# A top-32 attention and mixer kernel: sixty score blocks masked by an accumulating DMA, and one small VectorE step moved to GpSimd, in a newly planned order

## The chip, the core and the metric

The kernel runs on one core of a Trainium2 chip. The metric is device time in microseconds (us): the median of several executions. The engines are called PE (TensorE), DVE (VectorE), ACT (ScalarE), POOL (GpSimd) and SP (SyncE, which here only issues DMAs). Each works through its own list of instructions strictly in order; between engines they wait for each other by semaphores.

## What is computed

```python
scores = scale * np.matmul(q, k.transpose(0, 1, 3, 2))        # (8, 8, 576, 576)
kth = np.partition(scores, -32, axis=-1)[..., -32:-31]
scores = np.where(scores >= kth, scores, -1e9)                # keep the 32 largest of a row
attn = softmax(scores)                                        # with 1e-9 added to the sum
x = np.matmul(attn, v)  ->  (batch, seq, heads * 64)
h = np.maximum(x.T @ w_tok1, 0) @ w_tok2                      # mixing over tokens
u = x + h.T
out = u + np.maximum(u @ w_ch1, 0) @ w_ch2                    # mixing over channels
```

Batch 8, 8 heads, 576 tokens, head size 64, hidden sizes 256 (tokens) and 1536 (channels). The exact 32nd largest of each of 36,864 rows of 576 scores has to be found.

## The kernel before

**Tiles.** Heads go in 32 pairs. A pair's 2 x 576 rows make nine tiles of 128 rows, and two tiles make a duo, so there are 288 tiles in 144 duos, nine duos (`two(m)`) for each of 16 couples of pairs. A duo's scores are 128 partitions x 2 x 576.

**One duo (`scores`, `group`), in order of its data.** PE multiplies q and k into PSUM (L568, 16 matmuls). ACT copies the scores, scaled and shifted, into a buffer `SX` (L378). DVE takes the eight largest of each of seven segments of a row (L605, MAX8, fourteen for a duo) and merges them (L609, L610, L612) into a guess of the threshold, `thi`; `nh` is its negative (L705, a line that a helper `small` shares). ACT counts with the sign function how many scores lie above the guess (L621, into `cnt`). From the count come three small factors, 128x6 numbers each, all made on DVE at L705: `gs` (which side to search), `ws` (how far) and `as`, which is made from `ws`. POOL rewrites the scores in `SX` as whole numbers with `nh` and `gs` (L628, twice) and sets eight dummies behind each row with `as` (L631). One more DVE MAX8 over 584 numbers gives the exact threshold `tlo` (L637, twice), `nt` is its negative.

**Masking, in two ways.** 104 duos are "swap" duos: POOL writes a mask byte into `U` (L646, twice), PE adds it, made hugely negative, to a second computation of the scores in PSUM (L578 and L584, the "rescore"), and ACT takes the exponential out of PSUM into `Pm` (L651). The other 40 (the table `KEEP`, and every fifth duo of nine, whose rows come from both pairs) need no second computation: ACT takes the exponentials of the unmasked scores from `SX` early into `E` (L617), DVE makes two more small factors `no` (L659), POOL writes a mask of zeros and ones `M` (L663, twice) and multiplies (L668, twice) into `Pm`.

**Behind the mask.** SP issues a transposing DMA `Pm` to `PT` (L690); PE multiplies `PT` with v (L741); DVE divides by the row sums into `Xb` (L757, L760). When a batch's four pairs are done, `mlp_ops` runs its mixing on PE and ACT (L813 to L937, L889 for the last product, L907 for the copy out). PE fills some gaps with matmuls whose result nobody reads (`heat`, L1068). At the end `judge` and `sums` (DVE, L1030 to L1054) work out from counts and thresholds whether a slower exact path has to run; in these runs it doesn't.

**What sets the order.** Nothing is left to run time: `Plan.run` takes every operation with an engine, a duration, dependences, buffers and a due time (`DUE` and `SHIFT`, interpolated over the tiles) and lists, at build time, what stands when on each engine. The numbers in `DUE`, `SHIFT`, `TOL` and the durations in `plan.add` thus decide the order and nothing else.

**Buffers.** Ten `SX`, three `U`, eight `PT`, three `Pm`, two `E`, two `M`; PSUM has eight banks, a duo's scores or second scores hold four of them.

Of the kernel before, what the change touches and what calls it, by code (L numbers as in the profile page):

```python
# [31 lines left out]
KEEP = tuple(18 * m + 2 for m in range(16)) + tuple(18 * m + 14 for m in range(8))  # L32
# [4 lines left out]
    lq=-133.951, tq=-932.231, ck=-35.592, nh=237.787, vc=490.837, mm=-49.848, cp=-459.747, seg=521.49, rnd=1.494,  # L37
    sg=-30.872, g=136.538, a=154.386, w=-424.736, x=323.58, dum=1.612, mx=-190.096, nt=-286.048, u=-918.815,
    re=-1.774, ex=-191.301, ex1=16.779, tr=-511.689, pv=-52.864, nm=-625.622, mlp=94.104, seg1=-6.015, rnd1=278.031,
    x1=49.757, sg1=49.48, mx1=-334.781, pace=-2.756, mla=-161.079, first=-599.221, part=-502.53, rest=-442.515,  # L40
# [1218 lines left out]
```

## Time and profile before

| | |
|---|---|
| time, median of 3 runs | 753.7 us (753.56 to 754.14) |
| the profiled execution | 754.53 us, of which the core's span is 752.7 us |
| busy in the span | PE 709.1 us (94%), DVE 702.5 (93%), ACT 666.1 (88%), POOL 631.7 (84%) |
| TensorE clock granted | 0.997 of full speed over the span |
| DMA | 90.51 MB, mean 120 GB/s |

A busy time is the union of the times in which an engine had an instruction in flight. Instructions of one engine overlap, so the busy time of a group can be more than the engine's time that it costs; where that matters, starts of successive instructions are compared. The 1.8 us outside the span belong to every run.

### The profile page before, as it was taken

The numbers are of one execution on the slowest core, as the hardware profiler recorded it, in microseconds if no ns is written. First come the engines' busy times: TensorE is split into PE (matmuls) and PEld (weight loads), VectorE is DVE, ScalarE is ACT, GpSimd is POOL, SyncE is SP. The second block draws the span as 40 slices with busy tenths as digits, with TensorE's granted clock in tenths as the row PEclk, the third lists the DMA queues.
The fourth block names the chain that finished last, engine by engine and source line by source line (L and its number), as shares of the span: only waits on it lengthen the run. The fifth ranks groups of instructions, "written<-read, shape, count | busy, mean of one in ns | idle before, by whom it ended". The sixth has DMA issues, their size and how long they took to land.

```text
span 752.7 us, 23305 instructions
## 1 busy us (share of the span) xinstructions
PE 709.1 (94%) x7638; PEld 388.8 (52%) x7638; DVE 702.5 (93%) x4384; ACT 666.1 (88%) x1134; POOL 631.7 (84%) x859
## 2 busy tenths in 40 slices
PE   8888899999999999999999999999999999999995
PEld 3444545555555545554556555555555455555652
DVE  8999999999999999999999999999999999996620
ACT  5987989998999999999989999999998989997441
POOL 4799999999898999999997899999879897987300
PEclk9999999999999999999999999999999999999998
DMA  5865986975759557475676557688744747345521
GB/s 127 161 114 95 160 130 116 154 150 121 147 82 163 102 130 153 98 127 130 125 145 141 102 100 144 143 146 130 131 93 93 141 96 153 76 76 84 100 71 61
DMA packets 286722, 90.51 MB, mean 120 GB/s; under 512 B 273024, under 2 KB 283136, under 8 KB 286592
## 3 DMA queue, kind: packets, MB, share of 16 engines
q1 hardware_dynamic: 282768, 84.97, 59.5%
q0 software_dynamic: 3024, 3.77, 3.7%
q8 instruction: 62, 1.02, 0.6%
q14 instruction: 68, 0.56, 0.2%
q10 hardware_dynamic: 800, 0.20, 0.1%
HBM read 35.85 MB, written 9.44 MB: 60 GB/s over the span
## 4 chain that ended last, share of the span: by engine, by line
DVE 79%; PE 15%; ACT 2%; issue 1%; DMA 0%; SPq 0%; POOL 0%; ACTq 0%; POOLq 0%
DVE cd L605 34%; DVE tlo L637 23%; DVE cd L610 5%; PE bank L889 5%; DVE thi L612 4%; PE bank L937 3%; DVE m L609 3%; DVE Xb L760 2%; PE bank L584 2%; DVE nt L705 1%; DVE nh L705 1%; DVE ws L705 1%; PE bank L741 1%; ACT SX L378 1%; DVE as L705 1%
## 5 line engine op out<-in xcount | busy, mean ns | idle before, releaser
L605 DVE MAX8 cd<-SX 128x8 f32<-128x82 f32 (+1 forms) x2016 | 379.0, 231 | 1.9 <-ACT SX L378 1.7
L628 POOL TENSOR_SCALAR SX<-SX,nh,gs 128x576 int32<-128x576 f32 x288 | 234.7, 827 | 9.4 <-DVE as L705 3.8
L621 ACT ACTIVATE sg<-SX,nh 128x576 bf16<-128x576 f32 x288 | 223.1, 777 | 12.7 <-DVE nh L705 10.9
L637 DVE MAX8 tlo<-SX 128x8 uint32<-128x584 uint32 x288 | 219.0, 760 | 4.7 <-POOL SX L628 3.3
L646 POOL TENSOR_SCALAR U<-SX,nt,ws 128x576 uint8<-128x576 int32 x208 | 169.7, 831 | 22.0 <-DVE nt L705 5.4
L568 PE MATMUL bank<-kT,qT 64*64 64x288 f32 x2304 | 172.8, 414 | 11.4 <-ACT Pm L651 4.1
L378 ACT ACTIVATE SX<-bank 128x1152 f32<-128x1152 f32 (+1 forms) x147 | 161.1, 1108 | 14.7 <-PE bank L568 10.2
L651 ACT ACTIVATE Pm<-bank 128x1152 bf16<-128x1152 f32 x104 | 117.2, 1127 | 19.4 <-PE bank L584 18.0
L584 PE MATMUL bank<-kT,qT 64*128 64x288 f32 x832 | 129.0, 429 | 0.0
L568 PEld LDWEIGHTS bank<-kT,qT 64*64 64x64 f32 x2304 | 78.0, 132 | 81.2 <-ACT Pm L651 16.0
L668 POOL TENSOR_TENSOR Pm<-E,M 128x576 bf16<-128x576 bf16 x80 | 102.3, 1279 | 6.6 <-DMA PT<-Pm 0.3
L889 PE MATMUL bank<-wc2b,H 128*128 128x512 bf16 x384 | 91.3, 380 | 0.2
L937 PE MATMUL bank<-UT,wc1b 128*128 128x512 bf16 x380 | 90.0, 380 | 0.7 <-ACT Pm L651 0.5
L584 PEld LDWEIGHTS bank<-kT,qT 64*128 64x128 f32 x832 | 71.6, 186 | 33.5 <-issue 23.4
L663 POOL TENSOR_SCALAR M<-SX,no,ws 128x576 int8<-128x576 int32 x80 | 66.1, 827 | 15.2 <-DVE no L659 14.8
L937 PEld LDWEIGHTS <-wc1b 128*128 128x128 bf16 x380 | 34.0, 98 | 49.2 <-issue 15.3
L889 PEld LDWEIGHTS <-H 128*128 128x128 bf16 x384 | 34.7, 98 | 46.9 <-issue 13.1
L741 PEld LDWEIGHTS <-PT 128*128 128x128 bf16 x1600 | 52.3, 98 | 11.9 <-issue 7.8
L578 PE MATMUL bank<-U,identN 64*64 64x288 bf16 x832 | 47.7, 294 | 10.3 <-ACT SX L378 4.7
L621 ACT ACTIVATION_READ_ACCUMULATOR sg<-SX,nh 128x1 f32 x288 | 57.0, 198 | 0.0
L741 PE MATMUL bank<-vb,PT 128*128 128x65 bf16 x1600 | 54.8, 194 | 1.9 <-DMA PT<-Pm 1.0
L612 DVE MAX8 thi<-cd 128x8 f32<-128x42 f32 x288 | 54.6, 190 | 0.4
(124 smaller groups left out, 884.1 us busy)
## 6 DMA issues: line engine op xcount, KB each, us to landing
vL<-in_v_dram SPq DMA_DIRECT2D x64, 128.0 KB, 2.4
kL<-in_k_dram SPq DMA_DIRECT2D x63, 128.0 KB, 3.1
qL<-in_q_dram SPq DMA_DIRECT2D x62, 128.0 KB, 3.0
out_dram<-ob SPq DMA_DIRECT2D x14, 512.0 KB, 3.0
PT<-Pm SPq DMA_TRANSPOSE x143, 3.5
wc1b<-in_moe_w_ch_dram POOLq DMA_DIRECT2D x4, 384.0 KB, 6.0
wc2b<-in_moe_w_ch_dram POOLq DMA_DIRECT2D x4, 384.0 KB, 5.4
kL<-in_k_dram SPq DMA_DIRECT2D x32, 32.0 KB, 2.7
```

The lines of the kernel that those rows point to most:

```text
L378: nc.scalar.activation(out=dst, in_=src, func=AF.Copy, scale=GRID, bias=-LEVEL * GRID)
L568: nc.tensor.matmul(out=row(s1.t, h, lo, lo + HS, c, 64), lhsT=x["qT"].t[r, q0 : q0 + 64], rhs=x["kT"].t[r, lo : lo + HS], start=True, stop ...
L584: nc.tensor.matmul(out=row(s2.t, h, lo, lo + HS), lhsT=x["qT"].t[r, q0 : q0 + P], rhs=x["kT"].t[r, lo : lo + HS], start=False, stop=True)
L605: ss.append(plan.add("DVE", 0.146, due["seg"] + DUE["seg1"] * h, lambda a=a, h=h, cd=cd: nc.vector.max(cd.t[:, a, :], Sb.t[:, h, bounds[a] ...
L621: return [plan.add("ACT", 0.775, due["sg"] + DUE["sg1"] * h, lambda i=i0 + h, h=h: nc.scalar.activation(out=sg[:, h, :], in_=Sb.t[:, h, 0: ...
L628: xo.append(plan.add("POOL", 0.828, due["x"] + DUE["x1"] * h, lambda i=i0 + h, h=h: nc.gpsimd.tensor_scalar(out=xi(Sb)[:, h, 0:S], in0=Sb. ...
L637: mxs.append(plan.add("DVE", 0.69, due["mx"] + DUE["mx1"] * h, lambda i=i0 + h, h=h: nc.vector.max(tlo[:, at(i) - 7 : at(i) + 1], Sb.t[:, ...
L646: us.append(plan.add("POOL", 0.83, due["u"] + 0.01 * h, lambda i=i0 + h, h=h: nc.gpsimd.tensor_scalar(out=byte(U.t[:, h, :], 1), in0=xi(Sb ...
L651: oe = [plan.add("ACT", 1.02, due["ex"], lambda: nc.scalar.activation(out=Pm.t[:, :, 0:S], in_=pairs(s2.t), func=AF.Exp, scale=scale), [or ...
L741: nc.tensor.matmul(out=oo, lhsT=PT[g][0].t[:, 5 * h + j, :], rhs=vb.t[:, j, h, :], start=(j == 0), stop=(j == 4))
L889: nc.tensor.matmul(out=po, lhsT=H.t[:, fc, r0 : r0 + P], rhs=wc2b[:, fc, :], start=(fc == 0), stop=(rows is not None and fc == NF - 1))
L937: nc.tensor.matmul(out=o, lhsT=wc1b[:, cc, fc * P : (fc + 1) * P], rhs=UT.t[:, cc, :], start=(cc == 0), stop=(cc == (hi if whole else NC) ...
```

## The change

Four things change together.

1. The mask-and-multiply way goes, and with it `E`, `M`, `no` and `lift`. In its place stands an "add" way for 60 duos (the table `ADD`; each of them has an entry of its own there): ACT takes the exponentials straight from the first scores in PSUM into one of six new buffers `Pa`; POOL writes the same mask byte as for a swap duo into `U`; and a DMA issued by POOL adds `U` to the bits of `Pa` in place (as 16-bit integers, so that a dropped weight becomes zero). 84 duos stay swap duos. For each couple of pairs the nine duos hold 1 add duo (couples 0 and 1), 3 (2 to 8), 5 (9 to 12) and 6 (13 to 15, the last one 5); before, 3 of nine were kept in couples 0 to 7 and 2 in the rest.
2. `ws` is made by POOL (128x2 numbers) instead of DVE; `as` on DVE now waits for it.
3. `kT` gets 64 more columns (the last key block stands in front for one head), so that the weights of a duo are 2 x 576 columns without padding: transposing DMAs move nine blocks of 128 columns instead of ten. It takes one more PE transpose a pair, a copy of 640 instead of 576 columns, and one more v load a pair. The sign scratch `sg` becomes one byte an element; `judge` takes its scratch from `SX` and thereby waits for the last batch's normalised rows.
4. All planner numbers are new, so the order of every engine is new.

```diff
-KEEP = tuple(18 * m + 2 for m in range(16)) + tuple(18 * m + 14 for m in range(8))
+ADD = tuple(18 * m + k for m in range(16) for k in ((8,) if m < 2 else (2, 8, 12) if m < 9 else (2, 6, 8, 12, 16) if m < 13 else (2, 6, 8, 10, 12, 16)) if (m, k) != (15, 16))
...
-    slots("kT", 3, [P, S], f32)
+    slots("kT", 3, [P, S + ST], f32)
...
-    for name in ("nh", "gs", "as", "ws", "nt"):
-        slots(name, 10, [P, 6 * GMAX], i32 if name == "as" else f32)
-    slots("no", 4, [P, 12 * GMAX], f32)
-    sg = sbt("sg", [P, 2, S], bf16)
-    slots("E", 2, [P, 2, S], bf16)
-    Ms = slots("M", 2, [P, S], bf16)
+    for name, n, dt in (("nh", 6, f32), ("gs", 6, f32), ("as", 6, i32), ("nt", 6, f32), ("ws", 2, f32)):
+        slots(name, 10, [P, n * GMAX], dt)
+    sg = sbt("sg", [P, 2, S], i8)
     Us = slots("U", 3, [P, 2, S], bf16)
-    Ps = slots("Pm", 3, [P, 2, PW], bf16)
-    slots("PT", 8, [P, 10, P], bf16)
+    slots("Pm", 2, [P, 2, S], bf16)
+    slots("Pa", 6, [P, 2, S], bf16)
+    slots("PT", 8, [P, 9, P], bf16)
...
-            ox = plan.add("ACT", 1.2, t + DUE["ex1"], lambda: nc.scalar.activation(
-                out=E.t[:, :, :], in_=Sb.t[:, :, 0:S], func=AF.Exp, scale=scale / GRID, bias=lift[:, :]), ev, acq=[E], use=[Sb])
+            ox = plan.add("ACT", 1.011, t + DUE["ex1"], lambda: nc.scalar.activation(
+                out=Pm.t[:, :, :], in_=pairs(s1.t), func=AF.Exp, scale=scale), [om], acq=[Pm], use=[s1, Pm])
...
             else:
-                oe = []
-                no = Buf("no")
-                n = il + 1 - first
-                for h in range(2):
-                    M = Buf("M")
-                    oo = plan.add("DVE", 0.07, due["nt"] + 0.01, lambda i=i0 + h, h=h: nc.vector.tensor_scalar(
-                        out=no.t[:, 3 * n * h : 3 * n * h + 3 * n], in0=thrice(gs.t[:, 0:n]), scalar1=256.0,
...
-                    oe.append(plan.add("POOL", 1.37, due["u"] + 0.02 * h + 0.01, lambda h=h, M=M: nc.gpsimd.tensor_tensor(
-                        out=Pm.t[:, h, 0:S], in0=E.t[:, h, :], in1=M.t[:, :], op=ALU.mult), [ox, ou],
-                        acq=[] if h else [Pm], use=[E, M, Pm]))
+                od = plan.add("POOL", 0.66, due["ad"], lambda: nc.gpsimd.dma_start(
+                    out=Pm.t[:, :, :].rearrange("p h c -> p (h c)").bitcast(i16),
+                    in_=U.t[:, :, :].rearrange("p h c -> p (h c)"), accum_op=ALU.add), us + [ox], use=[U, Pm], dma=1.8, fly=2.7, lag=0.34)
+            oe = [od]
...
+        ow = plan.add("POOL", 0.36, due["w"], lambda: nc.gpsimd.tensor_scalar(
+            out=ws.t[:, 0:n], in0=some, scalar1=MIDDLE, scalar2=4.0, op0=ALU.add, op1=ALU.mult), every, acq=[ws], lat=0.06)
...
+        oa = plan.add("DVE", 0.055 + 0.0035 * n, due["a"], lambda: nc.vector.tensor_scalar(
+            out=as_.t[:, 0 : 3 * n], in0=thrice(ws.t[:, 0:n].bitcast(i32)), scalar1=0x7FFFFFFF, scalar2=18,
+            op0=ALU.bitwise_and, op1=ALU.logical_shift_right), [ow], acq=[as_], use=[ws])
...
-    jd = plan.add("DVE", 6.0, T * NT + 16.0, judge, lasts)
+    jd = plan.add("DVE", 6.0, T * NT + 16.0, judge, lasts + mixed[B - 1], acq=[space])
```

The line numbers of the new kernel are its own (L635 for L628, L644 for L637, L652 for L646, L592 for L584, L702 for `ws`, L662 for the mask's DMA, L624 for the exponential into `Pa`). What moves in the order is shown at three places.

DVE, from the last duo's `nh` to its last exact threshold, before. Here `ws`, `gs`, `as` are the factors, `no` the two extra factors of a kept duo, MAX `tlo` the long MAX8:

```order
L705 TENSOR_SCALAR ws_149<-cnt 128x6
L705 TENSOR_SCALAR gs_128<-cnt 128x6
L705 TENSOR_SCALAR as_143<-ws_149 128x6
L637 MAX tlo<-SX_97 128x8 x2
L705 TENSOR_SCALAR nt_163<-tlo 128x6
L637 MAX tlo<-SX_91 128x8
L757 RECIPROCAL rds<-bank 128x10
L637 MAX tlo<-SX_91 128x8
L760 TENSOR_TENSOR Xb_191<-bank,rds 128x2x5x64
L705 TENSOR_SCALAR nt_166<-tlo 128x6
L659 TENSOR_SCALAR no_170<-gs_131,nt_163 128x6 x2
L637 MAX tlo<-SX_92 128x8
```

And in the new kernel, from the last duo's merge on:

```order
L620 MAX thi<-cd_105 128x8
L697 TENSOR_SCALAR nh_119<-thi 128x6
L644 MAX tlo<-SX_93 128x8 x2
L704 TENSOR_SCALAR gs_128<-cnt 128x6
L710 TENSOR_SCALAR nt_149<-tlo 128x6
L706 TENSOR_SCALAR as_139<-ws_160 128x6
L644 MAX tlo<-SX_92 128x8
L749 RECIPROCAL rds<-bank 128x10
L752 TENSOR_TENSOR Xb_187<-bank,rds 128x2x5x64
L644 MAX tlo<-SX_92 128x8
L710 TENSOR_SCALAR nt_148<-tlo 128x6
```

Before, the segments of the last duo (SX_95) still came after these rows; in the new order all segments are done, only two long MAX8 and one normalisation stand between `nh` of the last duo and its own MAX8, and `judge` stands behind everything.

POOL, some ten duos before the end, before: a kept duo's masks and products between the whole numbers of its neighbours.

```order
L631 TENSOR_TENSOR SX_93<-as_143,kdum 128x2x8
L663 TENSOR_SCALAR M_174<-SX_92,no_170,ws_148 128x576
L668 TENSOR_TENSOR Pm_181<-E_173,M_174 128x576
L663 TENSOR_SCALAR M_175<-SX_92,no_170,ws_148 128x576
L668 TENSOR_TENSOR Pm_181<-E_173,M_175 128x576
L628 TENSOR_SCALAR SX_93<-SX_93,nh_120,gs_128 128x576 x2
```

In the new kernel, about as far from the end:

```order
L702 TENSOR_SCALAR ws_164<-cnt 128x2
L652 TENSOR_SCALAR U_167<-SX_96,nt_152,ws_161 128x576
L638 TENSOR_TENSOR SX_97<-as_143,kdum 128x2x8
L635 TENSOR_SCALAR SX_97<-SX_97,nh_124,gs_135 128x576 x2
L652 TENSOR_SCALAR U_168<-SX_97,nt_153,ws_164 128x576 x2
L662 DMA Pa_173<-U_168 128x1152
L702 TENSOR_SCALAR ws_165<-cnt 128x2
```

The products are gone, one DMA issue (L662) stands in their place, and every duo has one `ws` more in POOL's list.

PE, the last rescore (L578 and L584, now L586 and L592) and what follows it, before:

```order
L578 MATMUL bank<-U_178,identN 64x288
L584 MATMUL bank<-kT_89,qT_86 128x288 x4
L889 LDWEIGHTS H_196
L889 MATMUL bank<-wc2b,H_196 128x512
L889 LDWEIGHTS H_196
```

and in the new kernel:

```order
L586 MATMUL bank<-U_168,identN 64x288
L592 MATMUL bank<-kT_88,qT_85 128x288 x4
L929 LDWEIGHTS wc1b
L929 MATMUL bank<-UT_190,wc1b 128x512
L929 LDWEIGHTS wc1b
```

Before, eighteen matmuls of L889 and eight of L894 that belong to the seventh batch stood behind the last rescore; in the new order none of that batch does, and what stands there is the last batch's own.

## Rows read from the trace of the kernel before

**Rows 1.** Busy time of each engine by stretch of the span, in us from its start; then the granted clock, the DMA engines' mean share and GB/s. The first three lines are stretches of 40 us out of a longer answer, the last two the whole middle and the end.
```profile
300.00:340.00 40.00, 38.56 (x431) 21.00 (x431) 39.97 (x257) 39.56 (x71) 38.22 (x50) 1.00 0.60 121
580.00:620.00 40.00, 39.42 (x379) 19.95 (x378) 39.72 (x243) 36.05 (x64) 35.01 (x48) 1.00 0.57 114
620.00:660.00 40.00, 38.97 (x432) 21.77 (x428) 39.91 (x252) 37.52 (x65) 35.76 (x50) 1.00 0.58 118
...
20.00:680.00 660.00, 628.49 (x6944) 344.89 (x6936) 657.33 (x4199) 623.33 (x1061) 604.10 (x819) 1.00 0.68 125
680.00:753.00 73.00, 63.98 (x579) 35.68 (x577) 28.22 (x91) 31.17 (x53) 17.74 (x22) 0.97 0.35 74
```

**Rows 2.** The page's chain of work that ended last: shares of the span by engine.
```profile
DVE 79%; PE 15%; ACT 2%; issue 1%; DMA 0%; SPq 0%; POOL 0%; ACTq 0%; POOLq 0%
```

**Rows 3.** Groups of DVE instructions by line: count, busy us, mean ns of one, idle time before them and what ended it.
```profile
L637 DVE MAX8 tlo<-SX 128x8 uint32<-128x584 uint32 x288 | 219.0, 760 | 4.7 <-POOL SX L628 3.3 <-POOL SX L631 1.1
L705 DVE TENSOR_SCALAR ws<-cnt 128x6 f32<-128x6 f32 x144 | 20.4, 144 | 6.5 <-ACT sg L621 6.5
L659 DVE TENSOR_SCALAR no<-gs,nt 128x6 f32<-128x6 f32 x80 | 13.3, 206 | 0.0
```

**Rows 4.** DVE in order of time (start, duration): what `ws` and `no` take from one start to the next.
```profile
676.65 0.13 DVE L705 TENSOR_SCALAR ws<-cnt 128x6 f32<-128x6 f32 x1
676.71 0.14 DVE L705 TENSOR_SCALAR gs<-cnt 128x6 f32<-128x6 f32 x1
...
689.61 0.33 DVE L659 TENSOR_SCALAR no<-gs,nt 128x6 f32<-128x6 f32 x2
689.86 0.76 DVE L637 MAX8 tlo<-SX 128x8 uint32<-128x584 uint32 x1
```

**Rows 5.** Groups of POOL instructions, columns as in rows 3; DMA_DIRECT2D rows are the issue of a weight load on POOL.
```profile
L646 POOL TENSOR_SCALAR U<-SX,nt,ws 128x576 uint8<-128x576 int32 x208 | 169.7, 831 | 22.0 <-DVE nt L705 5.4 <-DVE no L659 3.5 <-DVE as L705 3.2
L668 POOL TENSOR_TENSOR Pm<-E,M 128x576 bf16<-128x576 bf16 x80 | 102.3, 1279 | 6.6 <-DMA PT<-Pm 0.3
L663 POOL TENSOR_SCALAR M<-SX,no,ws 128x576 int8<-128x576 int32 x80 | 66.1, 827 | 15.2 <-DVE no L659 14.8
L631 POOL TENSOR_TENSOR SX<-as,kdum 128x16 int32<-128x16 int32 x144 | 29.2, 215 | 10.2 <-DVE as L705 5.4 <-DVE gs L705 3.6 <-DVE nh L705 0.8
L420 POOL DMA_DIRECT2D wc2b<-in_moe_w_ch_dram x4 | 3.3, 817 | 0.0
L420 POOL DMA_DIRECT2D wc1b<-in_moe_w_ch_dram x4 | 2.4, 598 | 0.0
```

**Rows 6.** Groups of ACT instructions, the same columns.
```profile
L651 ACT ACTIVATE Pm<-bank 128x1152 bf16<-128x1152 f32 x104 | 117.2, 1127 | 19.4 <-PE bank L584 18.0 <-POOL SX L628 0.7
L617 ACT ACTIVATE E<-SX,lift 128x1152 bf16<-128x1152 f32 x40 | 50.2, 1254 | 0.5 <-POOL Pm L668 0.4
L548 ACT COPY kT<-bank 128x576 f32<-128x576 f32 x31 | 20.2, 651 | 0.4 <-PE bank L473 0.4
```

**Rows 7.** Groups of PE matmuls, the same columns.
```profile
L584 PE MATMUL bank<-kT,qT 64*128 64x288 f32 x832 | 129.0, 429 | 0.0
L578 PE MATMUL bank<-U,identN 64*64 64x288 bf16 x832 | 47.7, 294 | 10.3 <-ACT SX L378 4.7 <-ACT Pm L651 3.2 <-POOL U L646 1.9
L473 PE MATMUL bank<-identF,kL 128*128 128x128 f32 x155 | 22.2, 274 | 0.7 <-DMA kL<-in_k_dram 0.7
```

**Rows 8.** DMA queues (packets, MB, share of 16 engines' span), and issues with KB each and median us from issue to landing.
```profile
q1 hardware_dynamic: 282768, 84.97, 59.5%
q0 software_dynamic: 3024, 3.77, 3.7%
...
PT<-Pm SPq DMA_TRANSPOSE x143, 3.5
wc1b<-in_moe_w_ch_dram POOLq DMA_DIRECT2D x4, 384.0 KB, 6.0
...
w1b<-in_moe_w_tok_dram POOLq DMA_DIRECT2D x1, 256.0 KB, 4.5
```

**Rows 9.** DVE in order of time near the end; the bracket is idle time before an instruction and what ended it.
```profile
682.54 0.16 DVE L705 TENSOR_SCALAR ws<-cnt 128x6 f32<-128x6 f32 x1 [2.83 <-ACT sg L621]
...
685.59 1.64 DVE L637 MAX8 tlo<-SX 128x8 uint32<-128x584 uint32 x2 [2.69 <-POOL SX L628]
...
699.53 0.16 DVE L705 TENSOR_SCALAR ws<-cnt 128x6 f32<-128x6 f32 x1 [3.05 <-ACT sg L621]
...
702.73 0.31 DVE L1031 TENSOR_SCALAR ti<-cnt 128x288 int32<-128x288 f32 x1
...
709.11 0.16 DVE L1050 TENSOR_REDUCE bad<-bad 128x1 f32<-128x6 f32 x1
...
722.46 1.29 DVE L976 TENSOR_TENSOR H<-bank,SX 128x512 bf16<-128x512 f32 x2 [7.91 <-PE bank L971]
```

**Rows 10.** PE in order of time, from the last rescore (L584) to the last matmul.
```profile
705.97 1.24 PE L584 MATMUL bank<-kT,qT 64*128 64x288 f32 x8
707.14 1.47 PE L889 MATMUL bank<-wc2b,H 128*128 128x512 bf16 x6
708.44 0.39 PE L894 MATMUL bank<-identB,UT 128*128 128x128 bf16 x4
...
743.73 0.39 PE L894 MATMUL bank<-identB,Ut 128*128 128x128 bf16 x4
```

More of the change, by code (lines that the diff above doesn't have):

```diff
@@ L36 @@
 DUE = dict(
[L37 to L40, printed above, removed]
+    lq=-97.018, tq=-1540.901, ck=-736.352, nh=372.026, vc=415.668, mm=-107.462, cp=-386.626, seg=552.311,
@@ L109 @@
     STAY = 0.0
-    TOL = {"PE": 0.1903, "DVE": 0.0354, "ACT": 0.1437, "POOL": 0.0254, "SP": 0.5289}
+    TOL = {"PE": 0.2650, "DVE": 0.0325, "ACT": 0.2661, "POOL": 0.0545, "SP": 0.4709}
     def __init__(self):
@@ L640, in whole_numbers, with weights @@
             return mxs
[L642 to L649 removed]
+        def weights(first, il, nt, on, ws, ow):
+            us = []
+            for h in range(2):
+                us.append(plan.add("POOL", 0.81, due["u"] + 0.01 * h, lambda i=i0 + h, h=h: nc.gpsimd.tensor_scalar(
+                    out=byte(U.t[:, h, :], 1), in0=xi(Sb)[:, h, 0:S], scalar1=nt.t[:, il - i : il - i + 1],
+                    scalar2=ws.t[:, i - first : i - first + 1], op0=ALU.add, op1=ALU.mult),
+                    [on, ow], acq=[U] if h == 0 else [], use=[U, Sb, nt, ws]))
+            if swap:
@@ L719, in group @@
-        mxs = [o for d, x in zip(ds, sgn) for o in d[4](first, il, nh, gs, og, as_, oa, x)]
-        on = small("nt", nt, lambda: tli[:, at(il) : at(first) + 1], ALU.mult, -1.0, ALU.add, 0.0, mxs)
+        nh, gs, as_, nt, ws = Buf("nh"), Buf("gs"), Buf("as"), Buf("nt"), Buf("ws")
+        some = cnt[:, first : il + 1]
+        oh = plan.add("DVE", 0.055 + 0.0035 * n, due["nh"], lambda: nc.vector.tensor_scalar(
+            out=nh.t[:, 0 : 3 * n], in0=thrice(thi[:, at(il) : at(first) + 1]), scalar1=-1.0, scalar2=BETWEEN,
+            op0=ALU.mult, op1=ALU.add), tops[-n:], acq=[nh])
@@ new lines, in group @@
+        sgn = [d[2](il, nh, oh) for d in ds]
+        every = [o for x in sgn for o in x]
+        ow = plan.add("POOL", 0.36, due["w"], lambda: nc.gpsimd.tensor_scalar(
+            out=ws.t[:, 0:n], in0=some, scalar1=MIDDLE, scalar2=4.0, op0=ALU.add, op1=ALU.mult), every, acq=[ws], lat=0.06)
+        og = plan.add("DVE", 0.055 + 0.0035 * n, due["g"], lambda: nc.vector.tensor_scalar(
+            out=gs.t[:, 0 : 3 * n], in0=thrice(some), scalar1=-MIDDLE, scalar2=0.5, op0=ALU.is_lt, op1=ALU.subtract), every, acq=[gs])
@@ new lines, in group @@
+        oa = plan.add("DVE", 0.055 + 0.0035 * n, due["a"], lambda: nc.vector.tensor_scalar(
+            out=as_.t[:, 0 : 3 * n], in0=thrice(ws.t[:, 0:n].bitcast(i32)), scalar1=0x7FFFFFFF, scalar2=18,
+            op0=ALU.bitwise_and, op1=ALU.logical_shift_right), [ow], acq=[as_], use=[ws])
+        mxs = [o for d, x in zip(ds, sgn) for o in d[3](first, il, nh, gs, og, as_, oa, x)]
+        on = plan.add("DVE", 0.055 + 0.0035 * n, due["nt"], lambda: nc.vector.tensor_scalar(
+            out=nt.t[:, 0 : 3 * n], in0=thrice(tli[:, at(il) : at(first) + 1]), scalar1=-1.0, scalar2=0.0,
+            op0=ALU.mult, op1=ALU.add), mxs, acq=[nt])
```

304 lines of the change are left out of this document (142 added, 162 removed).

## The prediction

> **What bounds the kernel now.** I read the stretches first, since shares over the whole span mix the middle with the end. From 20 to 680 us DVE is busy 657.3 of 660 us; PE has 628.5, ACT 623.3, POOL 604.1 [rows 1]. The chain of waits says the same from the other side: 79% of it is DVE, 15% PE [rows 2]. The single stretches show how near the others stand: at 300 to 340 ACT has 39.6 of 40 us, at 580 to 620 PE has 39.4, and DVE misses at most 0.3 us in each [rows 1]. So for 660 us DVE's own work is the time, with three engines 5 to 8% behind it. After 680 the picture turns: DVE has 28.2 of 73 us and PE 64.0 [rows 1], where the last duos and the last batch's mixing run out. A change is worth what it takes from DVE in the middle, as long as no neighbour takes over, and what it takes from PE and from latencies at the end.
>
> **DVE.** Removed are 144 `ws` and 80 `no`; nothing is added in the middle. The grouped rows give 20.4 and 13.3 us busy [rows 3], 33.7 together, but these instructions overlap their neighbours. By starts, `ws` to the next instruction is 0.06 us, and two `no` take 0.25 [rows 4]: 144 x 0.06 = 8.6, 80 x 0.125 = 10.0, together **18.6 us**. I take starts, because an engine that is never idle is paid by starts; 33.7 is the other bound.
>
> **The new wait.** `as` now waits for POOL 144 times; before, it followed its producer on DVE itself. The nearest rows are DVE's waits for POOL before the long MAX8: 3.3 + 1.1 us for 288 of them [rows 3], 0.015 us each. For 144 that is **+2.2**; the bounds are nothing, and one whole POOL instruction of the smallest kind (0.215, rows 5) each time, 31 us. I take the low one because the planner puts other DVE work between `gs` and `as` as it did between POOL and MAX8. Queued behind a late `as` would be the segments of the next duo, and then everything.
>
> **POOL.** Out go the 80 products, 102.3 us. The 80 masks `M` become `U`, 0.827 against 0.831 us, nothing. In come 144 `ws` of 128x2: the nearest row in size is 128x16 with 0.215 us, so 31 us; the bounds are 0.19 x 144 = 27 by the overlap in that row's busy time (29.2 for 144 is 0.20) and, as if they were full rows, 0.83 x 144 = 120. In come 60 issues of a DMA: the issues of weights took 0.60 and 0.82 [all rows 5], so 36 to 49; I take 42. Sum: 631.7 - 102.3 + 31 + 42 = 602 us, less than before; with the upper bounds 698. In the middle POOL thus falls from 604 to about 575 of the new length, no bound.
>
> **ACT.** 40 exponentials from `SX` at 1.254 us go, 20 swap exponentials go, 60 exponentials from PSUM into `Pa` come; the last two kinds have one form, 1.127 us [rows 6]. That is -50.2 - 22.5 + 67.6 = -5.1. The `kT` copies grow by a ninth, 31 x 0.65 / 9 = +2.2. The signs keep their length whether they write one byte or two, as their input of 576 numbers is unchanged: 0, with no row for the other. So ACT has 620 us in a middle that is to become 660 - 16 = 644: 96%, against 94% before. This is what the gain stands on: ACT must lose 13 of its 37 idle us. I think it can, since part of these waits were for DVE's `nh` or for PE's products, and both engines get lighter.
>
> **PE.** Twenty rescores go: (129.0 + 47.7) / 104 = 1.70 us each [rows 7], -34. One transpose a pair comes, 31 x 0.14 = +4.4. PE is not the bound in the middle, so this is worth nothing there by itself, but it lets the seventh batch's mixing finish earlier. PSUM: an add duo holds its four banks for two ACT reads instead of one (+1.1 us, 40 duos), 20 duos spare a second set of banks (1.7 + 1.1 us): +44 - 56, about nothing.
>
> **DMA.** Transposes lose a tenth. 60 mask DMAs of 295 KB come. All plain queues spend 59.5% of 752.7 = 448 us for 85 MB, 5.3 us per MB; POOL's queue 3.7% = 28 us for 3.77 MB, 7.4 per MB [rows 8]. So one mask DMA costs 1.6 to 2.2 us of all 16 engines, and twice 2.2 if reading the destination costs a pass of its own; I take 2.2, 130 us in all, and 5 us to land (4.5 and 6.0 for 256 and 384 KB, rows 8), before a transpose that takes 3.5. Before, the two products took 2.6 us there. The late stretches with most add duos have a DMA share of 0.57 and 0.58 [rows 1]; six masks in some 40 us add 0.33, and 0.66 by the upper price. The delay is covered by six `Pa` and eight `PT`; where that cover goes, PE's L741 waits, and DVE's normalisation behind it.
>
> **The end.** Behind the last rescore PE runs from 707.1 to 744.1 without a pause. Eighteen L889 (three times 1.30) of the seventh batch stood there [rows 10] and no longer do: -3.9, of which I count 3.5 as some may become waiting. DVE waited 2.83 and 2.69 us between the last duos [rows 9]; in the new order that place is full of long MAX8. I count 4 of these 5.5, since `ws` on POOL lengthens the one wait that must remain, from the last `nh` to the last MAX8 (3.05 now). `judge`, 702.7 to 709.2 or 6.5 us, moves behind the last normalisation, where DVE idles 7.9 [rows 9]: 0, and up to 6.5 if the sum of the last batch gets shorter than it. Together **-7.5**.
>
> **Sum.** 754.5 (the profiled execution) - 18.6 + 2.2 - 7.5 = 730.6; the runs' median lies 0.8 below that execution, so **730 us**. If the end gives nothing it is 737; with no new wait and all 9.4 us of the end it is 726; below that the removals must be worth more than their starts, and their bound of 33.7 alone would give 715.
>
> **Rivals.**
> *ACT becomes the bound.* For it: 39.6 of 40 us in a stretch [rows 1], 19.4 us of waits for PE [rows 6], and that its work falls by 3 us only. Against it: ten `SX` between ACT and DVE. If ACT keeps its 37 idle us, the middle shrinks by 3 instead of 16; with the end unchanged in the sum that is 743, and with nothing gained at the end 751.
> *The mask DMA throttles POOL (slower).* Three `U` serve all duos, and POOL may not rewrite one before its mask DMA has read it. With 575 of 644 us POOL can lose 69 us in the middle, 1.15 per mask DMA. If a landing in a crowded queue takes 5 us longer than those rows and POOL waits half of it, POOL needs 575 + 150 = 725, and the time is about 815; at 1.6 us each it is 761. For it: the DMA share of 0.9 that I get late. Against: by the new order a `U` is rewritten some ten POOL instructions, about 6 us, after its DMA's issue.
> The issue itself can do the same. Issues of POOL took 0.60 to 0.82 us while DVE was never idle [rows 1, 5], so DVE did not hold them up; if each took 3 us, POOL would need 575 + 60 x 2.3 = 713 and the kernel some 800. The Trainium skill, page "SBUF — State Buffer", section "SBUF: two separate sides", warns of this: while DVE runs an instruction in its two-port mode, GpSimd can't write the descriptors of a DMA that it issues, and the transfer stands still. By that rule only the small DVE factors of this kernel could do harm, each for a moment; the trace with its 0.6 to 0.8 us doesn't show it.
> *The change is hidden.* `as` waits so often that the 18.6 us come back as waits of 0.13 each; then only the end gains: 746, or 753 with nothing there.
>
> **How the numbers follow.** My forecast, 722 to 738, gets 0.60; ACT as the bound, 739 to 751, 0.20; hidden, 746 to 753, 0.06, a third of it within 0.2%; POOL throttled, 755 and more, 0.09; better than 722 (the removals worth nearer to their busy time) 0.05. No change that this kernel's runs can tell is within 0.2%, 1.5 us. Faster: 0.60 + 0.20 + 0.05 + 0.03 = 0.88; same 0.03; slower 0.09. The range 718 to 745 leaves out the throttled POOL, half of the hidden case and the upper half of ACT's.
>
> **What would show it.** Right: no `ws` or `no` on DVE, DVE still at 99% or more of the middle, its last exact threshold some 25 us before 702; POOL's busy time near 600; mask issues near 0.7 us; no L889 of another batch after the last rescore; waits of DVE for POOL under 5 us. Wrong: idle time of DVE in the middle, ended by ACT (first rival), by POOL's `ws` (third), or by PE's L741 whose `PT` is late (DMA); POOL idle before `U` with a DMA as releaser (second).

## The result: 0.7% slower, and the profile after

The changed kernel takes 758.8 us (median of 12 runs, 756.1 to 761.9) against 753.8 us for the kernel before in the same series: a ratio of 1.0072, 95% interval 1.0054 to 1.0089. The forecast was 730 us with a range of 718 to 745. The profiled execution took 757.9 us, 756.1 of them the span. First the page of the changed kernel: busy time by engine, the granted clock in 40 slices, the queues.

```profile
PE 679.7 (90%) x7240; PEld 380.6 (50%) x7307; DVE 688.6 (91%) x4163; ACT 665.3 (88%) x1134; POOL 605.0 (80%) x981
...
PEclk9999999999999999999999969999989999999999
...
q1 hardware_dynamic: 264976, 80.29, 53.9%
q0 software_dynamic: 11664, 21.47, 17.3%
```

POOL's 605.0 us stand against 602 in the forecast. But two slices show a clock below 0.9, which the kernel before had nowhere ahead of its end. The stretches, columns as in [rows 1]:

```profile
300.00:340.00 40.00, 38.91 (x436) 21.81 (x438) 35.28 (x190) 36.31 (x62) 38.41 (x60) 1.00 0.83 167
420.00:460.00 40.00, 33.57 (x346) 19.13 (x347) 35.55 (x214) 35.65 (x59) 34.68 (x56) 0.83 0.87 155
20.00:680.00 660.00, 596.64 (x6515) 336.08 (x6566) 632.30 (x3888) 616.10 (x1049) 565.14 (x917) 0.98 0.75 141
680.00:756.00 76.00, 66.82 (x596) 36.27 (x602) 40.61 (x168) 37.13 (x68) 30.91 (x47) 0.98 0.48 102
```

DVE, idle for 2.7 of these 660 us before, is now busy for 632.3 of them, and at 300 to 340 and 420 to 460 it loses 4 to 5 us out of 40. No engine has taken its place: PE, ACT and POOL all have less to do than in [rows 1]. What DVE waits for between 20 and 680 us (total, times, longest), first in the kernel before, where two rows are the whole list, then in the changed one:

```profile
DVE tlo L637 <- POOL SX L628: 0.6, 1, 0.6
DVE ws L705 <- ACT sg L621: 0.6, 2, 0.3
```
```profile
DVE tlo L644 <- POOL SX L635: 9.6, 16, 2.6
DVE rds L749 <- PE bank L733: 6.1, 3, 3.3
DVE gs L704 <- ACT sg L628: 4.6, 7, 1.3
DVE cd L613 <- ACT SX L377: 2.6, 4, 1.1
DVE as L706 <- POOL ws L702: 0.5, 2, 0.3
```

Three engines end these waits, none of them alone; they come to 23.4 us. The last row is the wait that the change adds: 0.5 us.

An account of DVE's time up to the start of its last exact threshold (`tlo`) puts this in one line for each of seven runs. For each kind of DVE instruction (its operation and what it writes) I take the lower quartile of its times from start to next start as its **own** cost, and what lies above as **waiting** (this includes waits shorter than the overlap of two records, which the list of waits doesn't show). It is an estimate: with other groupings that keep what an instruction writes apart, the changed kernel has 20 to 22 us less own work than the kernel before and 29 to 31 us more waiting. The **tail** is from the start of the last threshold to the end of the span. In us:

| profiled execution | own | waiting | last threshold at | tail | at half clock before 700 |
|---|---|---|---|---|---|
| before | 663.6 | 38.3 | 701.8 | 50.8 | 0 |
| changed | 641.9 | 69.4 | 712.1 | 44.1 | 30.7 |
| e3: before without `ws`, `no` | 646.0 | 52.2 | 698.1 | 50.5 | 0 |
| e14: e3, ScalarE relieved | 645.3 | 48.1 | 693.3 | 51.2 | 3.4 |
| e2: changed, no masks | 641.9 | 60.6 | 703.2 | 44.3 | 23.9 |
| e15: changed, gaps filled | 642.0 | 62.0 | 704.8 | 44.0 | 0 |
| e16: e15, no masks | 642.5 | 55.8 | 698.9 | 44.2 | 0 |

The saving on DVE came (own work -21.7), the tail got shorter (-6.7), and 31.1 us more waiting ate both. The experiments ask where these 31 us are from.

### The profile page after: what moved, and what is told of

Its sections match the earlier page's. It is cut to its first block, busy times and chain, and to the rows that moved or that the text cites. A ratio compares the mean times of both kernels' runs of the same rounds, so it can differ in the third digit from the quotient of the medians.

```text
span 756.1 us, 22539 instructions
## 1 busy us (share of the span) xinstructions
PE 679.7 (90%) x7240; PEld 380.6 (50%) x7307; DVE 688.6 (91%) x4163; ACT 665.3 (88%) x1134; POOL 605.0 (80%) x981
## 5 line engine op out<-in xcount | busy, mean ns | idle before, releaser
L652 POOL TENSOR_SCALAR U<-SX,nt,ws 128x576 uint8<-128x576 int32 x288 | 240.8, 859 | 30.3 <-issue 10.4
L635 POOL TENSOR_SCALAR SX<-SX,nh,gs 128x576 int32<-128x576 f32 x288 | 245.3, 919 | 7.4 <-DVE gs L704 2.6
L628 ACT ACTIVATE sg<-SX,nh 128x576 int8<-128x576 f32 x288 | 224.1, 780 | 12.8 <-DVE nh L697 11.6
L644 DVE MAX8 tlo<-SX 128x8 uint32<-128x584 uint32 x288 | 219.3, 762 | 14.9 <-POOL SX L635 12.2
L658 ACT ACTIVATE Pm<-bank 128x1152 bf16<-128x1152 f32 x84 | 94.8, 1129 | 25.4 <-PE bank L592 23.9
L592 PE MATMUL bank<-kT,qT 64*128 64x288 f32 x672 | 107.9, 441 | 0.0
L881 PE MATMUL bank<-wc2b,H 128*128 128x512 bf16 x360 | 88.2, 380 | 3.1 <-issue 1.4
L592 PEld LDWEIGHTS bank<-kT,qT 64*128 64x128 f32 x672 | 59.6, 191 | 28.2 <-issue 19.1
L624 ACT ACTIVATE Pa<-bank 128x1152 bf16<-128x1152 f32 x60 | 67.8, 1130 | 0.0
L733 PEld LDWEIGHTS <-PT 128*128 128x128 bf16 x1600 | 54.1, 99 | 23.9 <-issue 20.6
L929 PEld LDWEIGHTS <-wc1b 128*128 128x128 bf16 x380 | 34.6, 99 | 50.1 <-issue 17.1
L586 PE MATMUL bank<-U,identN 64*64 64x288 bf16 x672 | 43.0, 299 | 16.5 <-ACT SX L377 7.6
L881 PEld LDWEIGHTS <-H 128*128 128x128 bf16 x384 | 34.9, 98 | 45.4 <-issue 11.8
L628 ACT ACTIVATION_READ_ACCUMULATOR sg<-SX,nh 128x1 f32 x288 | 57.6, 200 | 0.0
L702 POOL TENSOR_SCALAR ws<-cnt 128x2 f32<-128x2 f32 x144 | 27.4, 191 | 35.0 <-ACT sg L628 25.2
```

The source lines that it names most:

```text
L592: nc.tensor.matmul(out=row(s2.t, h, lo, hi), lhsT=x["qT"].t[r, q0 : q0 + P], rhs=keys(x, h, lo, hi), start=False, stop=True)
L628: return [plan.add("ACT", 0.762, due["sg"] + DUE["sg1"] * h, lambda i=i0 + h, h=h: nc.scalar.activation(out=sg[:, h, :], in_=Sb.t[:, h, 0: ...
L635: xo.append(plan.add("POOL", 0.81, due["x"] + DUE["x1"] * h, lambda i=i0 + h, h=h: nc.gpsimd.tensor_scalar(out=xi(Sb)[:, h, 0:S], in0=Sb.t ...
L644: mxs.append(plan.add("DVE", 0.68, due["mx"] + DUE["mx1"] * h, lambda i=i0 + h, h=h: nc.vector.max(tlo[:, at(i) - 7 : at(i) + 1], Sb.t[:, ...
L652: us.append(plan.add("POOL", 0.81, due["u"] + 0.01 * h, lambda i=i0 + h, h=h: nc.gpsimd.tensor_scalar(out=byte(U.t[:, h, :], 1), in0=xi(Sb ...
L658: od = plan.add("ACT", 1.011, due["ex"], lambda: nc.scalar.activation(out=Pm.t[:, :, :], in_=pairs(s2.t), func=AF.Exp, scale=scale), [orr] ...
```

## The experiments

### Half clock: e1, e5, e6, e15

The changed kernel's TensorE runs at half clock in five stretches, 30.7 us. The longest, with the stretch ahead of it (columns as above):

```profile
430.00:438.00 8.00, 5.11 (x63) 3.10 (x59) 7.86 (x44) 8.00 (x13) 7.71 (x13) 1.00 1.11 238
438.40:452.10 13.70, 11.16 (x76) 6.68 (x77) 10.67 (x68) 9.58 (x17) 10.75 (x18) 0.50 0.65 104
```

PE in order of time at this place (start, duration, idle time before and what ended it), and then ACT:

```profile
431.60 2.31 PE L576 MATMUL bank<-kT,qT 64*64 64x288 f32 x32
434.51 1.20 PE L576 MATMUL bank<-kT,qT 64*64 64x288 f32 x16 [0.60 <-ACT SX L377]
438.32 0.66 PE L586 MATMUL bank<-U,identN 64*64 64x288 bf16 x8 [2.61 <-ACT Pa L624]
...
442.43 2.20 PE L576 MATMUL bank<-kT,qT 64*64 64x288 f32 x16 [1.23 <-ACT Pm L658]
```
```profile
433.27 2.20 ACT L377 ACTIVATE SX<-bank 128x1152 f32<-128x1152 f32 x2
...
436.05 1.20 ACT L377 ACTIVATE SX<-bank 128x1152 f32<-128x1152 f32 x1
437.06 1.21 ACT L624 ACTIVATE Pa<-bank 128x1152 bf16<-128x1152 f32 x1
...
446.54 1.12 ACT L624 ACTIVATE Pa<-bank 128x1152 bf16<-128x1152 f32 x1
```

PE's scores stand in two sets of four PSUM banks. An add duo's set is free only when ACT has read it twice, for `SX` and for the exponential `Pa`, and by the order the second read comes late: 437.06 for one set, 446.54 for the other. So PE has no bank to write to and stands for 2.61 us, and the filling matmuls of the kernel, which need a free bank too, can't stand there either. Then the clock is at 1.2 instead of 2.4 GHz, and the same sixteen matmuls of a score take 2.20 us instead of 1.20. The Trainium skill, page "TensorE: Matmul & The Clock Gate", section "A second HAM failure mode: psum-queue depth-cycling", describes a kernel whose groups of matmuls cycle through PSUM banks with short idle spells between them, and whose clock goes up and down for it. The trace agrees: the stall is for a bank, and the granted clock behind it is 0.50.

**e1**: some 350 short matmuls into columns of PSUM that no score uses, in each gap up to the time at which a bank gets free (`hi`). Code cuts are shortened; `...` marks what is left out.
```
+ own = [b for b in rows if b.left or b.end >= hi]
+ if own and not early:
+     for j in range(int(0.8 * (hi - lo) / 0.11)):
...
+         f.fn = lambda c=own[-1].t[0]: self.spare(c)
...
+ def spare(c):
+     nc.tensor.matmul(out=bank[:, c : c + 224], lhsT=identB[:, :], ...)
```


> The changed kernel in its own order, with some 350 short matmuls (224 columns) that write to unused columns of PSUM put into the gaps of TensorE's order in which no bank was free for the existing filler. Theory CLOCK (the five stretches at half clock between 359.9 and 646 us, about 31 us together, begin behind gaps of TensorE of 1.6 to 2.6 us and cost VectorE 9 to 10 us of waits, 4.5 of them at 443 to 462): the granted clock stays at 1.0 up to the end and the time falls by 8 to 11 us, to 747 to 750. Theories MASK and ORDER (VectorE waits for GpSimd behind its mask issues, or where the new order makes it wait, and the clock falls because of that): 757 to 760, whatever the clock does.

Measured: 766.6 us, ratio 1.0161 (1.0147 to 1.0175), granted clock 0.997. The clock came back and the kernel got slower. The list of waits says why (L1075 is the added matmul):
```profile
PE bank L1075 <- ACT SX L388: 20.6, 16, 1.3
PE bank L1075 <- ACT Pm L669: 6.3, 6, 1.2
```
The added matmuls waited for ACT's read of the bank that they write beside. That they then stood in the way of the scores is my reading, no run parts it. For CLOCK this run is inconclusive. **e4**, the same without mask transfers, went the same way (761.9 us, ratio 1.0106, 1.0090 to 1.0121) and tells no more.

> The short matmuls of e1 and no mask transfers (60 duos unmasked, fallback kept from running), in the new order. If clock and masks are two separate losses: the sum of what e1 and e2 gain, 738 to 743. If the one causes the other: no better than the better of the two. What is left between this and 730 is then what the new order itself makes VectorE wait.

**e5**: as e1, but only into a bank whose last read is over and whose next read comes later; 60 matmuls in six gaps.


> The changed kernel in its own order, with 60 short matmuls that wait for nothing in six of TensorE's gaps, to unused columns of a bank that no engine is reading at that time: two gaps ahead of the stretch at half clock at 438 us, two ahead of the one at 554, one ahead of the one at 360, one at 258. (In e1 the 350 matmuls waited 27 us for ScalarE, so that run couldn't tell.) CLOCK: the stretches at 360, 438 and 554 (24 of the 31 us) become shorter or go, and the time falls by 4 to 8 us, to 750 to 754. Rival, the half clock costs nothing that would not be waited for anyway: 757 to 760 although the clock is back.

Measured: 755.3 us, ratio 1.0011 (0.9992 to 1.0031); half clock 13.6 us instead of 30.7. The direction is CLOCK's: 17 us less at half clock, 0.6% less time. The size, 3.6 us between the medians and 4.6 by the ratios, is at or below the low end of what was expected, and the time lies above the 750 to 754.

**e6**: the kernel before without its filling matmuls.
```
- for j in range(self.FIRST if early else int(0.8 * (st - t0 - 0.1) / d)):
+ for j in range(self.FIRST if early else 0):
```


> The kernel before in its own order, without the matmuls that fill TensorE's gaps (149 in its record; those of the first microsecond are left out too). It makes the gaps that the new order has in the kernel before. CLOCK: the granted clock falls to half behind gaps, some 20 to 60 us in all, and the time rises by 0.3 us for each us at half clock, as in the changed kernel (9 to 10 us of VectorE's waits for 31): 760 to 775. Rival, gaps do not lower the clock, or the lower clock is hidden: 753 to 756.

Measured: 758.3 us, ratio 1.0062 (1.0026 to 1.0097), half clock 34.1 us. (The nine fillers of the first microsecond stayed, unlike what the expectation says.) Gaps do lower the clock in the old order too, and it costs time, though with 0.14 us for each us at half clock half of what I had put, and so just below the 760 to 775 expected.

**e15**: as e5, in all 38 gaps; each matmul's bank is chosen by the reads planned for it.
```
+ own = [b for b in rows if all(e + 0.2 <= t or s > t + 0.11 for s, e in b.reads) and ...]
```


> The changed kernel in its own order with 287 short matmuls in 38 gaps of TensorE (e5 had 60 in six), each to unused columns of a bank that ScalarE has read at least 0.2 us earlier by the order's own times or reads later. Nothing is left out. CLOCK: all stretches at half clock but the last go (e5 left 13.6 of 30.7 us), and the time falls below e5's by 2 to 4 us, to 750 to 753, at or below the kernel before. Rival, the matmuls wait for ScalarE again and stand in the way as in e1: 757 to 766.

Measured: 750.7 us, ratio 0.9962 (0.9948 to 0.9975): nothing is left out in it, and it is faster than both kernels. The page's clock row, and two of the stretches that had lost most:
```profile
PEclk9999999999999999999999999999999999999999
```
```profile
300.00:340.00 40.00, 39.86 (x440) 22.34 (x436) 35.27 (x189) 36.18 (x62) 38.40 (x60) 1.00 0.83 163
420.00:460.00 40.00, 37.58 (x425) 22.28 (x427) 39.62 (x241) 39.43 (x67) 38.07 (x61) 1.00 0.93 168
```
At 420 to 460 DVE has 39.6 of 40 us instead of 35.6. So the half clock cost **8.1 us**, 0.26 for each of the 30.7. The single runs fit: the twelve of the changed kernel spread over 5.8 us, with granted clocks from 0.971 to 0.980; the five of e15, all at 0.998, lie within 0.3 us. At 300 to 340, where the clock was whole before too, nothing changes: DVE still loses 4.7 us, in two waits of 2.6 and 1.9 for POOL's `SX`.

### The mask transfers: e2, e7

POOL around an issue in the changed kernel, in order of time:
```profile
305.14 0.88 POOL L662 DMA_DIRECT2D Pa<-U  x1
305.74 0.53 POOL L638 TENSOR_TENSOR SX<-as,kdum 128x16 int32<-128x16 int32 x1
305.94 1.13 POOL L652 TENSOR_SCALAR U<-SX,nt,ws 128x576 uint8<-128x576 int32 x1
307.15 0.19 POOL L702 TENSOR_SCALAR ws<-cnt 128x2 f32<-128x2 f32 x1
307.44 0.82 POOL L652 TENSOR_SCALAR U<-SX,nt,ws 128x576 uint8<-128x576 int32 x1
```
The issue's record is 0.88 us (60 of them: 51.8, mean 0.863), and the next instruction starts 0.60 behind its start; but the two instructions behind it last 0.3 us longer than their like (0.53 against 0.21, 1.13 against 0.82). They start on time and end late, until POOL pauses: over all 60 issues the first three instructions behind one last some 0.25, 0.23 and 0.20 us longer (medians).

**e2**: the mask's issue is left out.
```
- lambda: nc.gpsimd.dma_start(out=Pm.t..., in_=U.t..., accum_op=ALU.add), us + [ox]
+ lambda: None, us + [ox]
```


> The changed kernel in its own order without the 60 mask transfers: nothing is issued or moved for them, so 60 duos go unmasked into the output; the fallback at the end is kept from running. Theory MASK (the 51.8 us of issues and some 40 us by which GpSimd's instructions behind an issue are longer end in VectorE's waits): GpSimd's busy time falls by about 90 us, VectorE's waits for GpSimd from 12 to 5 us or less, and the time to 745 to 751. Theories CLOCK and ORDER: less than 3 us, 755 to 759.

Measured: 750.3 us, ratio 0.9953 (0.9936 to 0.9969), **8.5 us** less. DVE's waits for POOL's `SX` fall from 9.6 to 4.3 us between 20 and 680 us. The time and the waits are MASK's; POOL's busy time fell by 49 us only (605.0 to 556.4), not by 90, as the longer records overlap. The profiled execution also had less half clock, 23.9 us against 30.7.

**e7**: the same issue for 2 columns.
```
- out=Pm.t[:, :, :] ..., in_=U.t[:, :, :] ..., accum_op=ALU.add
+ out=Pm.t[:, 0, 0:2] ..., in_=U.t[:, 0, 0:2], accum_op=ALU.add
```


> The changed kernel in its own order, its 60 mask transfers cut to 2 of 1152 columns, with the same issue and the same 128 rows (60 duos go unmasked into the output, the fallback is kept from running). It parts what e2 gained (8.5 us). If it is GpSimd's own work for the issue (0.86 us each, and the longer instructions behind it): still 756 to 759, and GpSimd's X steps behind an issue still take 1.05 us. If it is the data (288 KB beside the other transfers, 4.1 us until PT can start): 749 to 752, as e2.

Measured: 759.2 us, ratio 1.0067 (1.0046 to 1.0088), all of the loss. POOL's steps in e7 and in e2 (busy, mean ns of one):
```profile
L635 POOL TENSOR_SCALAR SX<-SX,nh,gs 128x576 int32<-128x576 f32 x288 | 246.1, 926 | 7.2 <-DVE gs L703 2.4
```
```profile
L635 POOL TENSOR_SCALAR SX<-SX,nh,gs 128x576 int32<-128x576 f32 x288 | 233.8, 821 | 7.0 <-DVE gs L702 3.0 <-DVE as L704 0.8
```
So the data cost nothing: with 0.5 KB instead of 288 the landing is faster (2.7 against 4.1 us) and the time the same. What is left is the issue on POOL or the 2.7 us until a landing, which e2 doesn't have either. The waits speak for POOL: DVE's for POOL's `SX` are 9.3 us in e7 and 4.3 in e2, while in the changed kernel and in e7 PE has no wait for a `PT` between 20 and 680 us.

### Does DVE bound the kernel before: e3, e13, e14, e10, e8

**e3** takes the prediction's first term alone, in the old order.
```
- wo[swap] = ws, small("w", ws, ...)
+ wo[swap] = ws, plan.add("DVE", ..., lambda: None, ...)
- lambda: nc.vector.tensor_scalar(out=no.t...)
+ lambda: None
```


> The kernel before in its own order, without VectorE's 144 ws and 80 no: their readers take constants, the step after ws reads the count itself (so it still waits for the sign row), M still waits for nt; the mask values are wrong, and the fallback at the end is kept from running. This is the first term of the prediction by itself, at the old order. If VectorE is what bounds the kernel before: minus 18.5 us (8.7 and 9.8 from start to start), to 734 to 737. If ScalarE, TensorE or GpSimd stand right behind it (ScalarE 623 of the 660 us from 20 to 680, against VectorE's 657): VectorE begins to wait, and the time falls by 8 to 13 us only, to 741 to 746.

Measured: 750.6 us, ratio 0.9954 (0.9938 to 0.9969): 3.5 us, less than either expectation. Own work falls by 17.6, as costed, and waiting rises by 13.9. The middle of e3 and DVE's waits in it:
```profile
20.00:680.00 660.00, 630.71 (x6968) 345.72 (x6970) 646.91 (x3983) 626.62 (x1068) 606.35 (x822) 1.00 0.68 125
```
```profile
DVE gs L705 <- ACT sg L623: 3.9, 5, 2.9
DVE rds L757 <- PE bank L741: 1.6, 1, 1.6
DVE tlo L639 <- POOL SX L630: 0.7, 1, 0.7
```

**e13** and **e14** relieve ScalarE, in the kernel before and in e3:
```
- out=sg[:, h, :], in_=Sb.t[:, h, 0:S]
+ out=sg[:, h, 0:HS], in_=Sb.t[:, h, 0:HS]
```


> The kernel before in its own order, with ScalarE relieved as in e11: its 288 sign rows read 288 of 576 columns (the counts and the masks that follow are wrong; the fallback is kept from running). The prediction took VectorE for the bound of the kernel before, since it stands 2.4 of the 660 us from 20 to 680. If VectorE alone bounds it: 752 to 754, no change, whatever ScalarE does. If the chain through ScalarE binds as well: 740 to 748.

> The kernel before with both reliefs: VectorE's ws and no left out as in e3 (750.6 us), and ScalarE's sign rows cut to half as in e13 (values wrong, the fallback kept from running). If e3 gained only 3.5 of VectorE's 11 us because ScalarE's chain stands right behind VectorE: now the whole 11 us and more come out, 738 to 743. If something else holds e3 (GpSimd, TensorE, the order): 747 to 751.

Measured: e13 752.4 us, ratio 0.9983 (0.9974 to 0.9992), 1.3 us; e14 745.8 us, ratio 0.9895 (0.9880 to 0.9911), 7.9 us. Relief of ScalarE alone is worth 1.3, of DVE alone 3.5, of both 7.9. So DVE is the first bound of the kernel before, and ScalarE's chain stands right behind it. It explains a part only: e14 lies between its two expectations and still waits 9.8 us more than the kernel before. All of this is at the old order; a new order planned for the lighter DVE might take out more.

**e10** moves `ws` alone to POOL, in the old order, and **e8** moves it back to VectorE, in the new one:
```
e10:
- small("w", ws, ...)
+ plan.add("DVE", ..., lambda ...: nc.gpsimd.tensor_scalar(out=ws.t..., in0=cnt..., ...), ...)
e8:
- lambda: nc.gpsimd.tensor_scalar(
+ lambda: nc.vector.tensor_scalar(
```


> One part of the change alone: the kernel before in its own order, with its 144 ws made on GpSimd at the place in the order where VectorE made them. By the prediction's terms: 8.6 us of VectorE's work go, 2.2 us of waits for GpSimd come: 746 to 749. By what e3 showed (of 11 us of work taken from VectorE 4 come out): minus 1 to minus 2 us, 751 to 753. Rival, GpSimd waits in its queue for the sign row and everything behind it is late: 756 to 765.

> The changed kernel with the factor of X made on VectorE again, at the same place in the order: 144 small instructions go from GpSimd (27.4 us, 25 us of waits for ScalarE ahead of them) back to VectorE. If VectorE bounds the changed kernel: slower by 5 to 8 us, 763 to 767. If VectorE mostly waits for others there: within 2 us of 758.8; if GpSimd bounds it: faster, 750 to 755.

Measured: e10 792.9 us, ratio 1.0512 (1.0498 to 1.0527); e8 771.0 us, ratio 1.0222 (1.0197 to 1.0246). Both beyond every expectation. In e10 the wait that the change adds is no longer small:
```profile
DVE as L705 <- POOL ws L716: 30.9, 61, 1.4
```
POOL's queue runs in order, and at DVE's old place a `ws` of 0.19 us stands behind instructions of 0.8. In the new order the same wait is 0.5 us. In e8 own work rises by 10.1 us (0.07 for each `ws`, to 652.0) and waiting by 4.0 (to 73.4). It also has 44.4 us at half clock against 30.7, which at 0.14 to 0.26 us each is 2 to 4 of its 12.2 us. The 8 to 10 left are about the work put on DVE, while of work taken from it (e3) a fifth came out. Taking `ws` from DVE is thus worth having, in an order made for it.

### What is left: e9, e12, e11, e16

**e9** is e5 without mask transfers, **e12** is e9 without POOL's V casts, **e11** is e9 with the sign rows halved as in e13 (0.54 instead of 0.78 us each).

> The changed kernel in its own order with the 60 short matmuls of e5 and without the mask transfers of e2 (60 duos go unmasked into the output, the fallback is kept from running). If mask issues and half clock are two separate losses: their sum, 8.5 and 4.6 us off 758.8, so 744 to 748. If one waits behind the other: 749 to 751, as e2. What VectorE still waits in it, beside the 15.5 us of the kernel before, is what the new order itself makes it wait: 8 to 12 us expected, at the places where it waits in the changed kernel too (312, 338, 595, 631, 671, 681 us).

Measured: 747.8 us, ratio 0.9909 (0.9894 to 0.9924), 2 us above the sum.

> As e9, without GpSimd's V casts from the fourth pair on (V of the first three pairs stands in for the rest; the fallback is kept from running). In e9 GpSimd stands 23 us at these casts, 6 times, up to 6.0 us, until TensorE's products free a vb, and everything behind in its queue stands too. If that is how the new order makes VectorE wait: 6 us or more come out, 738 to 742. If it is not: less than the 23 us of the casts would suggest, within 2 us of e9, 746 to 750.

Measured: 748.1 us, ratio 0.9927 (0.9908 to 0.9946): nothing. POOL stands at the V casts for 23 us and nobody pays for it.

> As e9 (60 short matmuls, no mask transfers, 747.8 us), and ScalarE relieved: its 288 sign rows read 288 of 576 columns, which takes some 0.24 us off each, 70 us in all (the counts, and all masks that follow from them, are wrong; the fallback is kept from running). It tells what VectorE's 15 us of waits that e9 has beyond the kernel before come from. If ScalarE's chain is what binds the new order (its waits in e9: VectorE for ScalarE's copies and signs 9 us, GpSimd for the signs 37 us): VectorE's idle time falls by 8 to 15 us, 732 to 740. If the order makes VectorE wait in other ways (GpSimd's queue behind the V cast, TensorE's products): less than 4 us, 744 to 748.

Measured: 737.3 us, ratio 0.9777 (0.9759 to 0.9796), 10.5 us less than e9. The middle of e9, then of e11:
```profile
20.00:680.00 660.00, 607.08 (x6638) 342.51 (x6697) 639.61 (x3932) 624.47 (x1065) 532.18 (x875) 0.99 0.59 119
```
```profile
20.00:680.00 660.00, 611.69 (x6755) 346.58 (x6817) 643.44 (x3974) 576.58 (x1078) 537.53 (x888) 0.99 0.60 120
```
ACT goes from 624 to 577 us and more work of DVE fits into the same 660 us. In the kernel before the same relief was worth 1.3 us; here it is 10.5, of which 1 to 2 may be clock (10.2 us at half clock against 17.1 in e9). ScalarE's chain has become a bound. One link of it is new: with `ws` on POOL, POOL's own queue stands for the sign rows, 35.5 us in e9 and 14.0 in e11; the kernel before has no such wait. Whether the gain is ACT's load or that each sign row ends sooner, the run doesn't tell.

**e16** is e15 without mask transfers.

> e15 (287 short matmuls, 750.7 us) without the mask transfers of e2 (60 duos go unmasked into the output, the fallback is kept from running). It closes the account: what is left between this and the predicted 730 belongs neither to the half clock (8.1 us by e15) nor to the mask issues (8.5 us by e2). If the two are separate: 741 to 744, and 11 to 14 us are left for the smaller saving on VectorE and the chain through ScalarE. If they overlap: 745 to 749, as e9.

Measured: 745.0 us, ratio 0.9885 (0.9869 to 0.9902). With the clock whole, the masks cost 5.7 us: half clock and masks cost 8.1 and 8.5 us alone and 13.8 together, so 2.8 us overlap. 15 us are left to the predicted 730. What DVE still waits for in e16 between 20 and 680 us:
```profile
DVE cd L628 <- ACT SX L392: 6.0, 6, 2.3
DVE tlo L659 <- POOL SX L650: 4.3, 5, 1.7
DVE gs L717 <- ACT sg L643: 3.5, 11, 0.8
DVE rds L762 <- PE bank L746: 0.7, 2, 0.4
DVE rds L762 <- ACT sg L643: 0.6, 2, 0.4
```
These are 15.1 us against 1.2 in the kernel before: ACT ends 10.1 of them, POOL 4.3 and PE 0.7.

## Why the prediction was wrong, step by step

- **DVE's saving** (18.6): right in size. e3 takes 17.6 off its own work, the changed kernel 21.7, some 3 of which are set-up work at the start.
- **"DVE's own work is the time"**: the step that failed first. Over 660 us DVE was idle for 2.7, and I read it as a bound with 5 to 8% of room behind it, where a saving comes out whole. In e3, at the old order, 14 of 17.6 us came back as waits. The room isn't one number: in single stretches [rows 1] ACT had 39.6 and PE 39.4 of 40. The first rival had named this ("ACT becomes the bound", 743 to 751, chance 0.20), and e16 lies there with 745.0. That is partly luck, as e16 is not the changed kernel and POOL ends 4.3 of its waits; but the rival deserved more than 0.20.
- **ACT** ("This is what the gain stands on: ACT must lose 13 of its 37 idle us"): it didn't. In the changed kernel ACT is idle for 43.9 of the 660 us, 7 more than before, and in e16 for 32, 5 less.
- **The new wait** (+2.2; third rival 0.13 each): 0.5 us in the new order, 31 us in the old, which was my upper bound. Its place in the order decides it.
- **POOL** (605.0 against 602): right as a sum, by errors of both signs: `ws` 27.4 for 31, issues 51.8 for 42, and longer records behind the issues that overlap their neighbours. Wrong was "no bound". The issues cost the kernel 5.7 to 8.5 us; POOL starts the next instruction 0.6 us after each, and what follows ends 0.2 to 0.3 us late, which DVE's thresholds wait for. The runs don't part these two. My second rival had the place, POOL held up by its own mask DMAs, but neither the mechanism nor the price (its 761 and 815 should also be 757 and 811 by the sum's own 86 us outside the middle): the waits before a `U` that the list puts down to no engine are 9.2 us in the changed kernel and 9.3 in e7, whose masks land 1.4 us sooner, so they were not for the landing; and no issue was near 3 us. By the Trainium skill, page "SBUF — State Buffer", section "SBUF: two separate sides", a VectorE instruction in its two-port mode could have held the issues up; 60 of them with a mean of 0.863 us and none above 1.16 don't show it.
- **DMA** (2.2 us each, landing 5): 288 KB land in 4.1 us, and e7 shows that the data cost nothing.
- **PE and PSUM** (-34 us of rescores, PSUM "+44 - 56, about nothing"): the sizes may stand, the sum was the wrong question. What counts is how long a set of banks stays taken until its second read, from 434.5 to 447.7 at the place shown, and that no filler can stand where no bank is free. I had not asked what the gaps of a lighter PE do to its clock: 8.1 us.
- **The end** (-7.5): two things in one term. The 3.5 for PE belong to the tail, which got 6.7 shorter; no L881 of an earlier batch stands behind the last rescore any more. The 4 for DVE's waits between the last duos stand in the waiting column: in the last 25 us ahead of the last threshold the listed waits fell from 9.7 to 4.8. Both came, the tail larger than forecast.

Together, from the account: the forecast had 1.8 us less waiting (+2.2 - 4), e16 has 17.5 more than the kernel before, which is 19.3 beyond it; clock and masks add 13.8; own work and the tail came out 3.1 and 3.2 better. That is 26.8 of the 28.8 us between 730 and 758.8. So clock and masks are more than the 5 us by which the change lost, and the largest part of the miss is waiting that the forecast put at less than nothing. Of the 17.5 us, the lists show 13.9: ACT ends 10.1 and POOL 4.3 of e16's waits. e11, where a lighter ACT gains 10.5 us, bears ACT's part out, though not with the clock whole. For POOL's part no run was made: what in its queue makes `SX` late stays open. An order made anew from the measured costs was not run either.
